# Loading the first 512 rows already transposed: the head of a fused attention and gate kernel

## The chip, the cores and the metric

The kernel runs on one core of a Trainium2 chip. The metric is the device time of one execution in microseconds (us). The engines that matter are TensorE (PE: matrix products; its weight loads are listed as PEld), VectorE (DVE), ScalarE (ACT), GpSimd (POOL), and SyncE (SP), which issues most DMAs. ACT issues some DMAs too; its DMA queue is called ACTq in the trace, that of SP SPq.

## The reference

A layer normalization of x (2048 rows of 512) feeds two branches: attention of 32 heads of 128 against cached keys and values, and a gated product. The two results are multiplied and added to x.

```python
xn = _layernorm(x, axis=-1)          # (x - mean) / sqrt(var + eps)
# A: q = xn @ wq ; softmax(q k^T / sqrt(128)) v ; @ wo            -> s
# B: gate = xn @ W_gate ; up = xn @ W_up                          (512 -> 1792)
#    h = gate * (gate > 0) * up ; h @ W_down                      (1792 -> 512)
# g = silu(B)
return x + s * g
```

All tensors are bfloat16. The weights of the gated branch have 1792 columns, that is 14 chunks of 128.

## The kernel before

The 2048 rows of x are handled as four quarters of 512 rows (Q = 0 to 3), each of four tiles of 128 rows. A matrix product on TensorE needs its inputs with the contracted dimension on the partitions, so x has to be transposed: 512 features as four blocks of 128 partitions.

The kernel starts with the gated branch of quarter 0. There are two ways to a transposed input. For quarter 0, in a hurry, the kernel uses the head: it only subtracts the mean, and puts the row factor 1/sqrt(var + eps) in later (r2 and r2h, line 571 and line 575, used after the down product: gate and up each carry one such factor, so the result carries its square). For the attention branch and the other quarters, VectorE takes statistics (`ln_stats`, line 419; `ln_aggr`, line 424), ACT the square root (`ln_sqrt`, line 431), VectorE the coefficients (`ln_coef`, lines 436 and 439), GpSimd normalizes (`ln_norm`, line 445), and SP transposes each normalized tile by DMA into `xnT` (line 557).

The order of all instructions is written out by hand; each engine works through its own list, and semaphores (`_wait`, `sig`) tie the lists together. No planner moves anything in this part.

At the start SP and ACT issue the loads: the four tiles of quarter 0 one by one (`load_x0`, line 328), the gate and up weights in four column groups (`load_w`, line 322, chunk limits 0, 2, 5, 9, 14), the other quarters of x (`load_xq`, line 332), and the down weights (line 350). TensorE meanwhile runs 18 products of ones with ones (`warm_mm`, line 475).

The head (`head_ln`, line 505) then goes tile by tile. For one tile: VectorE takes statistics and subtracts the mean (`head_center`, lines 450 to 454), TensorE transposes four blocks through PSUM (line 486 for the first tile, line 462 for the others), ACT copies them to `xcT` (line 493, line 467), and TensorE multiplies the tile with the first two weight chunks, gate and up, 16 matmuls of 128 columns (line 502 for the first tile, line 541 for the others).

The chunks 2 to 13 of quarter 0 follow in `emit_gate_up` (line 705): per chunk four matmuls of 512 columns for gate (line 729) and four for up (line 733); ACT applies the ReLU (line 689), VectorE multiplies (line 693), and `ln_task(fc)` (line 561) is called once for each chunk: it puts one piece of the statistics of the other quarters behind the product on VectorE. A chunk's PSUM banks come from a ring of three pairs (the pair of chunk 2 lies in the accumulator banks), and go back when VectorE's product has read them. Then comes the down product of quarter 0 (`emit_down`, line 832), which waits product by product for VectorE, the gate and up chunks of quarter 2, and the attention, which fills the rest of the time. When the last quarter is normalized, `issue_first` (line 373) issues the first keys, values and query weights on SP, behind the 16 transposes of line 557.

Of the kernel before, what the change touches and what calls it, by code (L numbers as in the profile page):

```python
# [8 lines left out]
ALU = mybir.AluOpType  # L9
# [43 lines left out]
def bass_recurrent_scan__mha_block_cached__glu_gated_reglu__prompt_kernel(  # L53
# [12 lines left out]
    _, S, D = A_x.shape  # L66
# [6 lines left out]
    QB = S // NQ  # L73
    NT = S // 128
    DC = D // 128
# [30 lines left out]
    x2 = A_x[0]  # L106
# [4 lines left out]
    pe = nc.tensor  # L111
# [5 lines left out]
    with ExitStack() as es:  # L117
# [201 lines left out]
        def load_w(eng, dst, src, sems, k):  # L319
            a, b_ = FCS[k] * 128, FCS[k + 1] * 128  # L320
            if b_ > a:
                sems[k].sig(eng.dma_start(dst[:, :, a:b_], src[:, :, a:b_]))

        x0_tok = {}
        x_tok = {}

        def load_x0(eng, n):
            x0_tok[n] = sem_x0[n].sig(eng.dma_start(x_sb[:, n:n + 1, :], x_t[:, n:n + 1, :]))

        def load_xq(Q):  # L330
            x_tok[Q] = sem_x[Q].sig(
                sp.dma_start(x_sb[:, 4 * Q:4 * Q + 4, :], x_t[:, 4 * Q:4 * Q + 4, :]))
# [40 lines left out]
        def issue_first():  # L373
            issue_kt(0)
            issue_wq(0)
            issue_v(0)
            issue_v(1)
            issue_wq(1)
            issue_wo(0)
            if NG > 1:  # L380
                issue_wo(1)
# [30 lines left out]
            ring_order.insert(1, s)  # L412

        def ln_stats(n):
            if n < 4:
                _wait(dve, x0_tok[n])
            elif n % 4 == 0:
                _wait(dve, x_tok[n // 4])
            return sem_ln1.sig(dve.bn_stats(stats[:, n, :], x_sb[:, n, :]))

        def ln_aggr(ns, stok):
            _wait(dve, stok)
            for n in ns:
                atok = sem_ln2.sig(dve.bn_aggr(mv[:, n, :], stats[:, n, :]))
            return atok

        def ln_sqrt(ns, atok):
            a, b_ = ns[0], ns[-1] + 1
            _wait(act, atok)
            return sem_sq.sig(  # L430
                act.activation(sqv[:, a:b_, :], mv[:, a:b_, 1:2], ACTF.Sqrt, bias=eps_sb[:]))
# [15 lines left out]

        xt_ready = {Q: [] for Q in range(QB)}

        def head_center(n):  # L450
            atok = ln_aggr([n], ln_stats(n))
            _wait(dve, atok)
            return sem_ln4.sig(
                dve.tensor_scalar(xc_sb[:, n, :], x_sb[:, n, :], mv[:, n, 0:1], None, op0=ALU.subtract))

        def head_transpose(n, ntok):
            tp_ps = acc_bf[n % 2]
            _wait(pe, acc_free[n % 2])
            _wait(pe, ntok)
            ins = None  # L460
            for c in range(DC):
                ins = pe.transpose(tp_ps[:, c * 128:(c + 1) * 128],
                                   xc_sb[:, n, c * 128:(c + 1) * 128], ident[:])
            ptok = sem_tp.sig(ins)
            src = tp_ps[:, 0:DC * 128].rearrange("p (c q) -> p c q", c=DC)
            _wait(act, ptok)
            acc_free[n % 2] = sem_xa.sig(act.copy(xcT[:, :, n * 128:(n + 1) * 128], src))
            return acc_free[n % 2]

        ones_w = nc.const_aps.tensor(1.0, [128, 128], BF16)  # L470
        ones_r = nc.const_aps.tensor(1.0, [128, 256], BF16)

# [1 line left out]
            for _i in range(k):  # L474
                pe.matmul(ps_r[:, 2 * NSLOT - 1, 0:256], ones_w, ones_r, start=True, stop=True)

        def head_first_transpose(ntok):
            toks = []
            for k in range(2):
                if k == 0:  # L480
                    _wait(pe, tok_pool)
                    _wait(pe, ntok)
                ins = None
                for i in range(DC // 2):
                    c = k * (DC // 2) + i
                    ins = pe.transpose(acc_bf[k][:, i * 128:(i + 1) * 128],
                                       xc_sb[:, 0, c * 128:(c + 1) * 128], ident[:])
                toks.append(sem_tp.sig(ins))
            for k in range(2):
                _wait(act, toks[k])  # L490
                src = acc_bf[k][:, 0:DC * 64].rearrange("p (c q) -> p c q", c=DC // 2)
                acc_free[k] = sem_xa.sig(
                    act.copy(xcT[:, k * (DC // 2):(k + 1) * (DC // 2), 0:128], src))
            return list(acc_free)

        def head_first_tile(k, i):
            W, sems = ((Wg_sb, sem_wg), (Wu_sb, sem_wu))[i]
            if k == 0:
                pe.wait_ge(sems[0].h, 16)
            for fc in range(HFC):  # L500
                for c in range(k * (DC // 2), (k + 1) * (DC // 2)):
                    pe.matmul(ps_r[:, 2 * half_slots[fc] + i, 0:128], W[:, c, fc * 128:(fc + 1) * 128],
                              xcT[:, c, 0:128], start=(c == 0), stop=(c == DC - 1))

        def head_ln():
            c0 = head_first_transpose(head_center(0))
            warm_mm(3)
            n1 = head_center(1)
            n2 = head_center(2)
            n3 = head_center(3)  # L510
            for _i in range(HFC):
                half_slots.append(ring_acquire())
            _wait(pe, c0[0])
            head_first_tile(0, 0)
            c1 = head_transpose(1, n1)
            head_first_tile(0, 1)
            _wait(pe, c0[1])
            head_first_tile(1, 0)
            head_first_tile(1, 1)
            c2 = head_transpose(2, n2)  # L520
            _wait(pe, c1)
            head_tile(1, 0)
            head_tile(1, 1)
            c3 = head_transpose(3, n3)
            _wait(pe, c2)
            head_tile(2, 0)
            head_tile(2, 1)
            _wait(pe, c3)
            head_tile(3, 0)
            head_tile(3, 1)  # L530

        half_slots = []

        def head_tile(n, fc):
            hs = slice(n * 128, (n + 1) * 128)
            fs = slice(fc * 128, (fc + 1) * 128)
            s = half_slots[fc]
            for i, W in enumerate((Wg_sb, Wu_sb)):
                ins = None
                for c in range(DC):  # L540
                    ins = pe.matmul(ps_r[:, 2 * s + i, hs], W[:, c, fs], xcT[:, c, hs],
                                    start=(c == 0), stop=(c == DC - 1))
                if n == 3:
                    half_tok[(fc, i)] = (sem_gate if i == 0 else sem_gu).sig(ins)
# [5 lines left out]
        def ln_finish(Q):  # L550
            ns, sqtok = ln_hold.pop("sq")
            ctok = ln_coef(ns, sqtok)
            for n in ns:
                ntok = ln_norm(pool, sem_nm, n, ctok)
                _wait(sp, ntok)
                xt_tok = sem_xq[Q].sig(
                    sp.dma_start_transpose(xnT[:, :, n * 128:(n + 1) * 128], xn_sb[:, n, :]))
            xt_ready[Q] = [xt_tok]
            return ctok

        def ln_task(i):
            if i < 4 * (QB - 1):
                if i == 1:
                    ns = list(range(4))
                    ln_hold["sq"] = (ns, ln_sqrt(ns, sem_ln2.cur()))
                ln_hold["st"] = ln_stats(4 + i)
                if i == 2:
                    ctok = ln_finish(0)
# [7 lines left out]
                if i % 4 == 3:  # L576
                    ns = list(range(i + 1, i + 5))
                    ln_hold["sq"] = (ns, ln_sqrt(ns, ln_aggr(ns, ln_hold["st"])))
                elif i >= 4 and i % 4 == 0:
                    ln_finish(i // 4)  # L580
            elif i == 4 * (QB - 1):
                ln_finish(QB - 1)
                issue_first()

        HS = S // 2
        HC = DC // 2
# [1457 lines left out]
```

## Time and profile before

| | us |
|---|---|
| median of 3 runs | 1241.56 (1241.18 to 1241.78) |
| the profiled execution | 1241.5 |
| its span, first to last instruction | 1239.9 |
| TensorE busy | 1232.4 (99%) |
| ACT busy | 1039.6 (84%) |
| VectorE busy | 876.3 (71%) |
| GpSimd busy | 729.8 (59%) |

The profile is one execution, taken by the hardware profiler. Its page gives the busy time of each engine, the span in slices, the DMA queues, the chain of work that ended last (followed back from the last instruction to what released each step), and the costliest groups of instructions. Further views answer questions: the timeline lists instructions in order (start, length, engine, line, operation, output and inputs, and in brackets how long the engine was idle before and who released it); the view of waits lists who waited for whom, with total, number of times and longest; the view of DMAs lists each issue with its size and the median time from its issue to its landing; the view of stretches gives busy times, granted clock, share of the DMA engines and GB/s of chosen stretches. Times in these rows are microseconds from the start of the span. Matmuls are pipelined: four that are listed with 1.03 us together follow the next ones 0.86 us later.

### The profile page before, as it was taken

To read this page: it belongs to the slowest core of one execution; us is meant where nothing else is said; L and a number is where in the kernel's file an instruction comes from. 1 tells how busy PE (TensorE), PEld (TensorE's weight loads), DVE (VectorE), ACT (ScalarE), POOL (GpSimd) and SP (SyncE) were. 2 spreads that over 40 slices of the span, in tenths; PEclk is the share of its full clock that TensorE was granted. 3 is DMA by queue.
4 is the path that set the end of the run, shared out by engine and by line. 5 is a ranking of instruction groups with operands and counts; after the bars stand their busy time and mean duration, and the time that the engine had idled before them with its cause. 6 is when DMAs were issued, how large, how long until landed. Compare 5 with 4: busy or idle time off the path is not lost.

```text
span 1239.9 us, 29084 instructions
## 1 busy us (share of the span) xinstructions
PE 1232.4 (99%) x11933; PEld 817.3 (66%) x11933; DVE 876.3 (71%) x1314; ACT 1039.6 (84%) x1108; POOL 729.8 (59%) x839
## 2 busy tenths in 40 slices
PE   9999999999999999999999999999999999999998
PEld 5466666776666666666666666666666666666664
DVE  6668788667676767676776777676677677675587
ACT  3457877668898998989989999989998999989994
POOL 3355876313757556745866566846765576662367
PEclk9999999999999999999999999999999999999999
DMA  9712431323222332233122322234222232238526
GB/s 276 157 31 37 79 79 23 52 48 98 53 49 52 65 70 52 48 69 63 38 35 52 73 61 53 48 69 69 48 52 57 39 56 48 52 69 141 112 37 143
DMA packets 279027, 85.38 MB, mean 69 GB/s; under 512 B 253552, under 2 KB 278896, under 8 KB 278896
## 3 DMA queue, kind: packets, MB, share of 16 engines
q1 hardware_dynamic: 277120, 82.08, 34.2%
q8 instruction: 95, 1.56, 0.6%
q10 hardware_dynamic: 1776, 1.44, 0.4%
q14 instruction: 36, 0.29, 0.1%
HBM read 36.96 MB, written 4.19 MB: 33 GB/s over the span
## 4 chain that ended last, share of the span: by engine, by line
PE 96%; POOL 1%; DVE 1%; issue 1%; DMA 0%; ACT 0%; POOLq 0%; DVEq 0%
PE ps_acc L1676 37%; PE ps_r L1567 35%; PE ps_r L1050 5%; PE ps_r L1167 3%; PE ps_r L1406 3%; PE ps_r L1228 3%; PE ps_r L1466 2%; PE ps_r L914 2%; PE ps_r L729 2%; PE ps_r L733 2%; PE ps_acc L832 1%; PE ps_r L1497 1%; PE ps_r L1498 0%; POOL gT L1755 0%; POOL s_acc L1533 0%
## 5 line engine op out<-in xcount | busy, mean ns | idle before, releaser
L1579 ACT ACTIVATE PT<-ps_r 128x1024 bf16<-128x1024 f32 x1024 | 988.7, 1025 | 129.6 <-PE ps_r L1567 117.5
L1676 PEld LDWEIGHTS ps_acc<-V_sb,PT 128*128 128x128 bf16 x8192 | 545.1, 98 | 231.1 <-issue 29.6
L1676 PE MATMUL ps_acc<-V_sb,PT 128*128 128x129 bf16 x8192 | 632.2, 220 | 0.0
L1567 PE MATMUL ps_r<-QT_sb,KT_sb 128*128 128x512 bf16 x2048 | 605.1, 379 | 0.2 <-DVE s_acc L1386 0.2
L1055 DVE TENSOR_TENSOR UVR<-UVR,ps_r 128x512 f32<-128x512 f32 (+1 forms) x228 | 168.7, 756 | 85.2 <-PE ps_r L1050 83.0
L1376 DVE TENSOR_TENSOR s_acc<-s_acc,ps_r 128x1024 f32<-128x1024 f32 x130 | 156.8, 1219 | 32.6 <-PE ps_r L1406 22.5
L1567 PEld LDWEIGHTS ps_r<-QT_sb,KT_sb 128*128 128x128 bf16 x2048 | 161.2, 98 | 26.4 <-DVE UVR L1055 4.3
L1015 POOL TENSOR_TENSOR TI<-xn_sb 128x512 f16<-128x512 f16 x48 | 55.9, 1165 | 97.0 <-PE ps_r L1050 97.0
L1384 DVE TENSOR_TENSOR s_acc<-s_acc,ps_r 128x512 f32<-128x512 f32 x116 | 77.4, 686 | 22.0 <-PE ps_r L1466 17.8
L1599 DVE TENSOR_TENSOR Onorm<-ps_acc,rz_sb 128x512 bf16<-128x512 f32 x127 | 87.8, 692 | 4.4
L1055 DVE TENSOR_TENSOR QT_sb<-UVR,ps_r 128x512 bf16<-128x512 f32 x72 | 49.5, 688 | 52.8 <-PE ps_r L1050 50.4
L1596 DVE RECIPROCAL rz_sb<-ps_acc 128x4 f32<-128x4 f32 x127 | 23.1, 182 | 82.7 <-PE ps_acc L1676 82.1
L1434 POOL TENSOR_TENSOR TI<-OX 128x512 f16<-128x512 f16 x28 | 31.8, 1156 | 65.1 <-issue 65.1
L1015 POOL TENSOR_TENSOR TI<-xnT 128x512 f16<-128x512 bf16 x36 | 41.6, 1156 | 39.7 <-PE ps_r L1050 21.4
L1322 POOL TENSOR_TENSOR WX<-Wo_sb 128x512 f16<-128x512 bf16 x7 | 8.1, 1155 | 90.4 <-DVE Wo_sb L1312 51.3
L1015 POOL TENSOR_TENSOR TI<-xn_sb,TI 128x512 f16<-128x512 f16 x48 | 56.0, 1167 | 0.0
L1123 POOL TENSOR_TENSOR QT_sb<-UVR,UVR 128x512 bf16<-128x512 f32 x24 | 29.8, 1277 | 39.9 <-DVE UVR L1055 39.9
L1050 PE MATMUL ps_r<-TI,SI 128*128 128x512 f16 x126 | 47.8, 379 | 0.0
L1123 POOL TENSOR_TENSOR UVR<-UVR,UVR 128x512 f32<-128x512 f32 x24 | 29.8, 1275 | 25.0 <-DVE UVR L1055 25.0
L1015 POOL TENSOR_TENSOR TI<-xnT,TI 128x512 f16<-128x512 bf16 x36 | 41.7, 1159 | 0.0
L1143 POOL TENSOR_SCALAR gB<-gB 128x512 bf16<-128x512 bf16 x14 | 20.8, 1485 | 30.4 <-DVE gB L1173 30.4
L1434 POOL TENSOR_TENSOR TI<-OT_store 128x512 f16<-128x512 bf16 (+1 forms) x28 | 32.1, 1170 | 8.7 <-issue 8.0
(229 smaller groups left out, 1357.8 us busy)
## 6 DMA issues: line engine op xcount, KB each, us to landing
V_sb<-in_A_v_cache_dram SPq DMA_DIRECT2D x32, 512.0 KB, 4.1
Wq_sb<-in_A_wq_dram SPq DMA_DIRECT2D x16, 256.0 KB, 3.1
Wo_sb<-in_A_wo_dram SPq DMA_DIRECT2D x8, 512.0 KB, 4.6
out_dram<-g_sb SPq DMA_DIRECT2D x4, 512.0 KB, 4.5
OT_store<-Onorm SPq DMA_TRANSPOSE x127, 2.5
Wd_sb<-in_B_W_down_dram SPq DMA_DIRECT2D x1, 1792.0 KB, 14.0
W<-in_B_W_gate_dram SPq DMA_DIRECT2D x14, 128.0 KB, 2.4
W<-in_B_W_up_dram SPq DMA_DIRECT2D x14, 128.0 KB, 2.8
```

The costliest lines, as they stand in the source:

```text
L1015: return sem_ui.sig(pool.tensor_tensor(dst, x, y, o))
L1050: return sem_up.sig(pe.matmul(dst, lhs, rhs, start=start, stop=stop, skip_group_check=True))
L1055: dve.tensor_tensor(dst, x, ps, ALU.add))
L1123: u_tok["add"] = u_tok[("add", i)] = sem_uv.sig(pool.tensor_tensor(dst, UU[:, i, :], RR[:, i, :], ALU.add))
L1167: ins = pe.matmul(ps_r[:, bank, :], L(i), R(i), start=(i == 0), stop=(i == HC - 1))
L1376: t = sem_opa.sig(dve.tensor_tensor(dst, dst, sb, op))
L1384: t = dve.tensor_tensor(dst, dst, sb, op)
L1434: return sem_oi.sig(pool.tensor_tensor(dst, x, y, o))
L1567: ins = pe.matmul(ps_r[:, 2 * s + tt, :], KT_sb[h % 2][:, t * 128:(t + 1) * 128], QT_sb[qt_slot[(h, Q)]][:], start=True, stop=True)
L1579: act.activation(PT[pb][:], ps_r[:, 2 * s:2 * s + 2, :], ACTF.Exp, scale=scale / WSC)
L1599: dve.tensor_tensor(Onorm[ob][:], o_ap, rz_sb[:].to_broadcast([128, 4, Dh]), ALU.mult))
L1676: ins = pe.matmul(o_ap, PT[pb][:, tt, j * 128:(j + 1) * 128], V_sb[vb][:, t, 0:VW], start=(t == 0 and j % 2 == 0), stop=(t == KT - 1 and j ...
```

## The change

The first 512 rows no longer come as rows for VectorE to centre. SP issues four DMA transposes, 128 rows each, from x in DRAM straight into `xcT`. TensorE multiplies each tile with a matrix of ones (four matmuls that add up in PSUM), which puts the sum over the features of each row on all partitions, and one VectorE instruction adds -1/512 of it to the tile in place. The 16 transposes on TensorE and the copies on ACT are gone, and so is the special path of the first tile. ACT now issues the first two groups of gate and up weights and then the 512 rows of x in the usual layout, which are still needed for the statistics. These statistics are moved into `ln_task`, between the chunks, where all the pieces get new places.

```diff
-        load_x0(sp, 0)
-        load_x0(act, 1)
-        load_w(sp, Wg_sb, wg_src, sem_wg, 0)
-        load_w(act, Wu_sb, wu_src, sem_wu, 0)
-        load_x0(sp, 2)
-        load_x0(sp, 3)
-        load_w(sp, Wg_sb, wg_src, sem_wg, 1)
-        load_w(sp, Wu_sb, wu_src, sem_wu, 1)
+        def load_x0t(n):
+            ts = slice(n * 128, (n + 1) * 128)
+            t0_tok.append(sem_x0[n].sig(sp.dma_start_transpose(xcT[:, :, ts], x2[ts, :])))
...
+        for n in range(4):
+            load_x0t(n)
+        for k in range(2):
+            load_w(act, Wg_sb, wg_src, sem_wg, k)
+            load_w(act, Wu_sb, wu_src, sem_wu, k)
+        load_xq(0, act)
         load_xq(1)
...
+        def head_center(n):
+            ts = slice(n * 128, (n + 1) * 128)
+            bank = n % 2
+            m_ps = ps_acc[:, bank, 0:128]
+            _wait(pe, acc_free[bank])
+            _wait(pe, t0_tok[n])
+            ins = None
+            for c in range(DC):
+                ins = pe.matmul(m_ps, ones_w, xcT[:, c, ts], start=(c == 0), stop=(c == DC - 1))
+            _wait(dve, sem_tp.sig(ins))
+            acc_free[bank] = sem_ln4.sig(
+                dve.scalar_tensor_tensor(xcT[:, :, ts], m_ps.unsqueeze(1).to_broadcast([128, DC, 128]), -1.0 / D,
+                                         xcT[:, :, ts], op0=ALU.mult, op1=ALU.add))
+            return acc_free[bank]
 
         def head_ln():
...
+            _wait(pe, tok_pool)
+            c = [head_center(0)]
             warm_mm(3)
+            c.append(head_center(1))
             for _i in range(HFC):
                 half_slots.append(ring_acquire())
+            for k in range(2):
+                pe.wait_ge((sem_wg, sem_wu)[k][0].h, 16)
+            for n in range(4):
+                _wait(pe, c[n])
+                head_tile(n, 0)
+                head_tile(n, 1)
+                if n < 2:
+                    c.append(head_center(n + 2))
...
         def ln_task(i):
+            for n in ((0,), (1,), (2, 3), (4,), (5,), (6,), (7,), (8, 9), (10,), (11,), (12,), (13,), (14, 15), ())[i]:
+                ln_hold["st"] = ln_stats(n)
+                if n % 4 == 3:
+                    ns = list(range(n - 3, n + 1))
+                    ln_hold["ag", n // 4] = (ns, ln_aggr(ns, ln_hold["st"]))
+            if i in (4, 8, 11, 13):
+                ns, atok = ln_hold.pop(("ag", (4, 8, 11, 13).index(i)))
+                if i == 4:
+                    _wait(act, warm_tok)
+                ln_hold["sq"] = (ns, ln_sqrt(ns, atok))
+            if i in (5, 9, 12, 13):
+                Q = (5, 9, 12, 13).index(i)
+                ctok = ln_finish(Q)
+                if Q == 0:
                     _wait(dve, ctok)
...
+                if Q == QB - 1:
+                    issue_first()
```

More of the change, by code (lines that the diff above doesn't have):

```diff
@@ L322, in load_w, with load_xq @@
                 sems[k].sig(eng.dma_start(dst[:, :, a:b_], src[:, :, a:b_]))
-        x0_tok = {}
         x_tok = {}
-        def load_x0(eng, n):
-            x0_tok[n] = sem_x0[n].sig(eng.dma_start(x_sb[:, n:n + 1, :], x_t[:, n:n + 1, :]))
-        def load_xq(Q):
-            x_tok[Q] = sem_x[Q].sig(
-                sp.dma_start(x_sb[:, 4 * Q:4 * Q + 4, :], x_t[:, 4 * Q:4 * Q + 4, :]))
-        load_x0(sp, 0)
-        load_x0(act, 1)
-        load_w(sp, Wg_sb, wg_src, sem_wg, 0)
-        load_w(act, Wu_sb, wu_src, sem_wu, 0)
-        load_x0(sp, 2)
-        load_x0(sp, 3)
-        load_w(sp, Wg_sb, wg_src, sem_wg, 1)
-        load_w(sp, Wu_sb, wu_src, sem_wu, 1)
+        t0_tok = []
+        def load_x0t(n):
+            ts = slice(n * 128, (n + 1) * 128)
+            t0_tok.append(sem_x0[n].sig(sp.dma_start_transpose(xcT[:, :, ts], x2[ts, :])))
+        def load_xq(Q, eng=sp):
+            x_tok[Q] = sem_x[Q].sig(
+                eng.dma_start(x_sb[:, 4 * Q:4 * Q + 4, :], x_t[:, 4 * Q:4 * Q + 4, :]))
+        for n in range(4):
[4 more added lines that the diff above has]
+        load_xq(0, act)
         load_xq(1)
@@ L414, in ln_stats @@
         def ln_stats(n):
-            if n < 4:
-                _wait(dve, x0_tok[n])
-            elif n % 4 == 0:
+            if n % 4 == 0:
                 _wait(dve, x_tok[n // 4])
@@ L448, in bass_recurrent_scan__mha_block_cached__glu_gated_reglu__prompt_kernel @@
         xt_ready = {Q: [] for Q in range(QB)}
[L450 to L468, printed above, removed]
         ones_w = nc.const_aps.tensor(1.0, [128, 128], BF16)
@@ L475, in warm_mm @@
                 pe.matmul(ps_r[:, 2 * NSLOT - 1, 0:256], ones_w, ones_r, start=True, stop=True)
[L477 to L503, printed above, removed]
+        def head_center(n):
[12 more added lines that the diff above has]
+            return acc_free[bank]
@@ L575, in ln_task @@
                         dve.tensor_scalar(r2h[:], r2[:], 0.5 / YSC, None, op0=ALU.mult))
[L576 to L583, printed above, removed]
+                if Q == QB - 1:
+                    issue_first()
         HS = S // 2
```

29 lines of the change are left out of this document (removed).

## The prediction

> **What bounds the kernel now.** First the page: span, busy times and the chain that ended last.
>
> ```profile
> span 1239.9 us, 29084 instructions
> PE 1232.4 (99%) x11933; PEld 817.3 (66%) x11933; DVE 876.3 (71%) x1314; ACT 1039.6 (84%) x1108; POOL 729.8 (59%) x839
> PE 96%; POOL 1%; DVE 1%; issue 1%; DMA 0%; ACT 0%; POOLq 0%; DVEq 0%
> ```
>
> TensorE is busy 1232.4 of 1239.9 us and carries 96% of the chain: whatever shifts TensorE's start shifts the end by as much, as long as no later wait opens. The profiled execution took 1241.5 us (1.6 us outside its span); the median of the three runs, 1241.56 us, is the same for this purpose, so I add the change to 1241.5.
>
> Second, that chain in the first 80 us, and who kept TensorE waiting there (columns: start, length, what; then engine, line, releaser, total, times, longest).
>
> ```profile
> 0.72 2.98 DMA x_sb<-in_A_x_dram
> 9.17 1.79 PE ps_r L541 x32
> 10.96 0.86 PE ps_acc L729 x4
> 31.68 12.09 PE ps_acc L832 x56
> ...
> PE ps_acc L486 <- DVE xc_sb L454: 0.7, 1, 0.7
> PE ps_acc L462 <- DVE xc_sb L454: 0.2, 1, 0.2
> ```
>
> After the head, TensorE waits for nobody: chunks 2 to 13 of the gate run back to back, 12 x 1.73 = 20.7 us from 10.96 to 31.68, then the 56 matmuls of the down product. Only the head has slack to win, and its prices are in the timeline of the first 12 us.
>
> ```profile
> 1.15 0.47 ACTq L322 DMA_DIRECT2D Wu_sb<-in_B_W_up_dram  x1
> 0.76 3.71 PE L475 MATMUL ps_r<-const-bfloat16-1.0 128*128 128x256 bf16 x18 [0.76 <-PEq L2029]
> 3.72 0.69 DVE L419 BATCH_NORM_STATS2 stats<-x_sb 128x6 f32<-128x512 bf16 x1 [3.72 <-DMA x_sb<-in_A_x_dram]
> 4.67 0.35 DVE L454 TENSOR_SCALAR xc_sb<-x_sb,mv 128x512 bf16<-128x512 bf16 x1
> 5.17 0.38 PE L486 MATMUL ps_acc<-ident,xc_sb 128*128 128x128 bf16 x4 [0.70 <-DVE xc_sb L454]
> 5.47 0.65 ACT L493 COPY xcT<-ps_acc 128x256 bf16<-128x256 bf16 x2 [2.33 <-PE ps_acc L486]
> 5.90 0.40 PE L502 MATMUL ps_r<-xcT,Wg_sb 128*128 128x128 bf16 x4
> 6.79 0.59 ACT L467 COPY xcT<-ps_acc 128x512 bf16<-128x512 bf16 x1 [0.67 <-PE ps_acc L462]
> 10.80 1.03 PE L729 MATMUL ps_acc<-xcT,Wg_sb 128*128 128x512 bf16 x4
> 11.03 0.69 DVE L693 TENSOR_TENSOR hT<-gr_sb,ps_r 128x512 bf16<-128x512 bf16 x1 [2.39 <-PE ps_r L541]
> ```
>
> The head ends at 10.80, when the full-width chunk starts. Before that the first tile goes landing 3.72, statistics, centering, transposes 5.17, copy 5.47, product 5.90: 2.2 us.
>
> **The change, step by step.**
>
> Removed: four statistics/centering groups (DVE), 16 transposes (TensorE), five copies (ACT). Added: 16 matmuls with ones, of the transposes' size (0.38 for four, pipelined; I take 0.25 in a stream), and four DVE subtractions from PSUM. The subtraction is not in the trace. Ends: 0.35 (the old centering, SBUF only) and 0.69 (L693, the same 128x512 with one PSUM operand); it has that PSUM operand, so 0.69. From landing to a usable tile this is 0.25 + 0.1 + 0.69 = 1.05 us, 1.1 less than the 2.2. The tiles' products stay: 32 in 1.79 us, so 0.9 us per tile of 16.
>
> So everything hangs on when the four transposes land. Their nearest rows: SBUF transposes of the same 128x512 (line 557: min/median/max of the issue in ns, then landing in us), and transposes beside a big transfer of ACT's queue at the kernel's end.
>
> ```profile
> L557 SPq DMA_TRANSPOSE xnT<-xn_sb x16: 1264/1265/5744, 15.9 to 41.7; - x16
> DMA to landing us min/median/max: 2.5/2.6/10.7
> ...
> FO<-gT SPq DMA_TRANSPOSE x2, 2.5
> ...
> 1230.04 0.40 ACTq L1723 DMA_DIRECT2D out_dram<-FO  x1
> 1230.39 1.93 SPq L1719 DMA_TRANSPOSE FO<-gT  x1
> ```
>
> The DMA rows that go with it, the loads' rows, and stretches (bounds in us, busy time of the five engines, granted clock, share of the DMA engines, GB/s):
>
> ```profile
> out_dram<-FO ACTq DMA_DIRECT2D x1, 512.0 KB, 3.9
> FO<-gT SPq DMA_TRANSPOSE x1, 4.1
> ...
> Wu_sb<-in_B_W_up_dram SPq DMA_DIRECT2D x1, 512.0 KB, 8.5
> Wu_sb<-in_B_W_up_dram ACTq DMA_DIRECT2D x1, 256.0 KB, 3.8
> Wg_sb<-in_B_W_gate_dram SPq DMA_DIRECT2D x1, 256.0 KB, 4.1
> Wd_sb<-in_B_W_down_dram SPq DMA_DIRECT2D x1, 1792.0 KB, 14.0
> ...
> 1.00:2.00 1.00, 1.00 (x7) 0.69 (x6) 0.00 (x0) 0.35 (x1) 0.51 (x4) 1.00 0.19 37
> 2.00:3.00 1.00, 1.00 (x6) 0.74 (x5) 0.00 (x0) 0.99 (x2) 0.00 (x0) 1.00 0.86 251
> ...
> 4.50:10.80 6.30, 5.38 (x84) 4.76 (x85) 3.90 (x11) 2.88 (x6) 0.00 (x0) 1.00 1.09 337
> 1130.00:1135.00 5.00, 5.00 (x55) 3.47 (x54) 2.56 (x4) 4.43 (x6) 3.04 (x3) 1.00 1.19 217
> ```
>
> A lone transpose costs SP 1.27 us and lands 2.5 us after its issue began. The one issued at 1230.39, beside a 512 KB transfer that ACT had issued 0.35 us earlier, held SP 1.93 us and landed after 4.1. In the changed kernel ACT issues 256 + 256 + 384 + 384 + 512 KB at once, 1.83 MB, which at the 337 GB/s of that stage is 5.4 us of full DMA: the transposes run in just that company. Ends for them: 1.27 apart and 2.5 to land (7.0 for the fourth: 0.72 + 3 x 1.27 + 2.5), or waiting until ACT's queue is empty (below). I take the row with a big neighbour for all but the first, whose issue starts before any packet flows: issues at 0.72, 1.99, 3.92, 5.85, landings at about 4, 6.1, 8.0, 9.95.
>
> TensorE's order (written by hand) is: mean 0, three warm-ups, mean 1, wait for both weights, tile 0, mean 2, tile 1, mean 3, tile 2, tile 3. The weights are issued at 0.71 and 1.15 on ACT and land at about 5.0 (0.47 us of issue each, 3.8 to land, as before). Then: warm-up to 4.47; mean 0 to 4.85, subtraction to 5.6; mean 1 waits for 6.1, to 6.35; tile 0 to 7.3; mean 2 waits for 8.0, to 8.3; tile 1 to 9.2; mean 3 waits for 9.95, to 10.2; tile 2 to 11.1; tile 3, whose subtraction ended at 11.0, to 12.0. That is 12.0 against 10.80: **+1.2 us**. Each mean in TensorE's queue holds the tile behind it, although that tile's own operands are ready.
>
> With the undisturbed landings the same walk ends at 9.75 (-1.05), because then tiles follow each other from 5.65.
>
> Statistics of the first 512 rows move into the chunks, with the x they read loaded last on ACT. Here DVE's rhythm decides:
>
> ```profile
> 20.00 0.69 DVE L419 BATCH_NORM_STATS2 stats<-x_sb 128x6 f32<-128x512 bf16 x1
> 20.60 0.67 DVE L693 TENSOR_TENSOR hT<-gr_sb,ps_r 128x512 bf16<-128x512 bf16 x1
> 23.10 0.38 DVE L424 BATCH_NORM_AGGREGATE mv<-stats 128x2 f32<-128x6 f32 x4
> ...
> ACT sqv L431 <- DVE mv L424: 7.3, 3, 2.8
> 4.91 1.15 SPq L322 DMA_DIRECT2D Wu_sb<-in_B_W_up_dram  x1
> 12.06 1.42 SPq L350 DMA_DIRECT2D Wd_sb<-in_B_W_down_dram  x1
> ```
>
> DVE starts one such operation every 0.6 us. After the first product it owes 13 products and 16 statistics (29 x 0.6 = 17.4), four aggregations (0.5 each) and the coefficient pairs (1.6): 21 us. With the head's end at 12.0 it begins near 12.8 and is through by 33.8; the last product is needed by the fourteenth down matmul, at 12.0 + 20.7 + 13 x 0.216 = 35.5. So it costs nothing, hidden by 1.7 us of slack; with a late x it would be next in line. ACT's three waits for aggregations (7.3 us) go, but they cost TensorE nothing and give nothing back. GpSimd normalizes the quarters later, SP's 16 transposes of them (1.27 each) then end near 44 instead of 43, before the differences on DVE need them at 46.2.
>
> Loads: the first 512 rows are fetched twice, 0.52 MB more, 1.6 us of DMA at 337 GB/s for all behind, and SP reaches its other loads only after the fourth transpose, at 7.8. Before, the third weight group was in by 13.4 (4.91 + 8.5). Now SP's next x and this group (1.57 MB, 4.7 us) are in by about 14, and chunk 5 needs it at 10.96 + 3 x 1.73 = 16.1, or later with a later head. The down weights landed at 26.1 (12.06 + 14.0), come 1.6 later, and are needed at 31.7. Covered; without that cover the 1.6 would show. ACT's table load slips behind five issues, to about 3, and ACT has nothing to do before 11.
>
> **Weighed against the skill.** The Trainium skill, Advanced Engine Details and Errata, section X-Bar Transpose (TRN2), calls transposing DMAs as fast as plain ones, 350 to 400 GB/s; transposes from DRAM at 1130 to 1135 moved 217. By the page the four would take 1.5 us of DMA instead of 2.4, an estimate that changes only the last rival.
>
> **Rivals.**
>
> Fair sharing. If the transposes share the DMA engines evenly with the weights, all 0.52 + 1.31 MB are through 5.4 us after the first packets (about 2.1: 37 GB/s flow from 1 to 2 us, 251 from 2 to 3), and the fourth lands near 8.0. Mean 3 ends at 8.3, its subtraction at 9.1, tile 3 at 10.0: -0.8 us, **1240.7**. For it: Wg on SP and Wu on ACT, issued together, took 4.1 and 3.8 us, an even split. Against it: the 4.1 us transpose. The Trainium skill, DMA: Bandwidth & Descriptors, section Queues, rings and completion order, has each DMA engine take packets from the queues in turn; by that this case would hold, and the even split agrees, the late transpose hardly.
>
> Starved transposes (the other side). If the 1230.39 row means that a transpose moves only when ACT's queue has drained, ACT's 1.83 MB keep it until 2.1 + 5.4 = 7.5; then four at 217 GB/s, 0.6 us each, land at 8.6, 9.2, 9.8, 10.4. Mean 0 ends at 8.9, tile 0 starts at 9.75, and with means and tiles behind each other tile 3 ends at 13.85: +3.05 us, **1244.55**. TensorE then idles from 4.85 to 8.65; its first 18 matmuls of 256 columns took 3.71 us, 0.206 each, where 512 columns later take 0.216, so a fall back to that pace for the next 3.4 us adds up to 2.5: 1247. It decides from a fourth landing of about 11.2, or from a fallback.
>
> The shorter path buys nothing: with weights landing at 5.9 instead of 5.0, tile 0 would start where it did, and even undisturbed transposes would save only what the tiles behind it wait less, some 0.8 us; that gives 1240.7 too and is counted with sharing.
>
> **How the numbers follow.** Likeliest (0.38): 1241.5 + 1.2 = 1242.7, own range 1241.7 to 1244.2, a twentieth of all chances beyond the bound. Sharing 0.22; starved 0.33; a stall opened later by DVE or a load, over 2.5 us, 0.05; an unforeseen gain 0.02 (the head allows no more than 1.75: 16 means and 64 products at 0.056 after weights at 5.0). About 0.2%, 2.5 us, is what a measurement of this kernel can tell from no change. Faster 0.02, same 0.33 + 0.22 = 0.55, slower 0.05 + 0.33 + 0.05 = 0.43. The range runs from just under the sharing case to within the starved one: 1240.4 to 1246.4.
>
> **What would show it.** Right: the third and fourth transposes held 1.9 us on SP and landing about 4 us after issue; TensorE waiting for them before means 1 to 3; the full-width chunk at 12.0; the chunks after it again 20.7 us without waits; subtractions of 0.69. Wrong: landings of 2.5 (then 9.75 to 10.0), landings only after x on ACT's queue (then 13.85), or a wait of TensorE on DVE or a load in the chunks.

## The result, and the profile after

| | before | after |
|---|---|---|
| median of six runs each, same chip, us | 1241.59 (1241.18 to 1241.78) | 1247.69 (1246.27 to 1248.48) |
| the profiled execution, us | 1241.5 | 1246.27 |
| its span, us | 1239.9 | 1244.8 |

The kernel became slower: ratio 1.0048, 95% interval 1.0037 to 1.0059, some 6 us. The prediction was 1242.7 with a range up to 1246.4. The profiled execution of after is the fastest of its six runs, so its trace accounts for 4.9 us of span. The page of after says the same of the bound as that of before: span, busy times, and the chain that ended last.

```profile
span 1244.8 us, 29080 instructions
PE 1234.4 (99%) x11933; PEld 818.9 (66%) x11933; DVE 876.4 (70%) x1314; ACT 1037.5 (83%) x1103; POOL 730.3 (59%) x839
PE 94%; POOL 2%; SPq 1%; DMA 1%; DVE 1%; issue 1%; ACT 0%; POOLq 0%; DVEq 0%; ACTq 0%
```

TensorE is still the bound, busy 2.0 us longer, though it has the same number of instructions. The rest is waiting, and the view of TensorE's waits in the first 80 us (total, times, longest) says for whom.

```profile
PE ps_acc L462 <- DMA xcT<-in_A_x_dram: 3.5, 2, 1.8
PE ps_r L682 <- DVE hT L646: 0.4, 1, 0.4
```

The timeline of the head shows where these lie (start, length, what; in brackets the idle time before and its cause).

```profile
0.72 5.23 SPq L329 DMA_TRANSPOSE xcT<-in_A_x_dram  x4
0.76 4.00 PE L452 MATMUL ps_r<-const-bfloat16-1.0 128*128 128x256 bf16 x18 [0.76 <-PEq L1982]
2.87 0.60 ACTq L333 DMA_DIRECT2D x_sb<-in_A_x_dram  x1
...
6.59 0.58 PE L462 MATMUL ps_acc<-xcT,const-bfloat16-1.0 128*128 128x128 bf16 x4 [1.84 <-DMA xcT<-in_A_x_dram]
7.21 0.69 DVE L465 SCALAR_TENSOR_TENSOR xcT<-ps_acc,xcT 128x512 bf16<-128x512 f32 x1 [7.21 <-PE ps_acc L462]
9.43 0.61 PE L462 MATMUL ps_acc<-xcT,const-bfloat16-1.0 128*128 128x128 bf16 x4 [1.61 <-DMA xcT<-in_A_x_dram]
9.83 0.63 PE L493 MATMUL ps_r<-xcT,Wg_sb 128*128 128x128 bf16 x4
10.26 0.63 PE L493 MATMUL ps_r<-xcT,Wu_sb 128*128 128x128 bf16 x4
12.68 0.39 PE L493 MATMUL ps_r<-xcT,Wg_sb 128*128 128x128 bf16 x4
12.90 0.39 PE L493 MATMUL ps_r<-xcT,Wu_sb 128*128 128x128 bf16 x4
15.20 1.03 PE L682 MATMUL ps_acc<-xcT,Wg_sb 128*128 128x512 bf16 x4
```

The first full-width chunk starts at 15.20 instead of 10.80: **4.40 of the 4.9 us are lost in the head.** TensorE waits for the first transpose until 6.59 and for the second until 9.43. After that it never waits again in the head, but from 9.83 to about 12.4 four matmuls of 128 columns follow each other every 0.43 us (9.83, 10.26) and only then every 0.22 (12.68, 12.90). Most of the longer busy time comes from this.

The view of DMAs gives the time from issue to landing. The transposes are rows 1, 2, 3 and 6 (issued at 0.72, 2.08, 3.38 and 4.68).

```profile
xcT<-in_A_x_dram SPq DMA_TRANSPOSE x1, 5.7
xcT<-in_A_x_dram SPq DMA_TRANSPOSE x1, 7.3
xcT<-in_A_x_dram SPq DMA_TRANSPOSE x1, 7.9
Wu_sb<-in_B_W_up_dram ACTq DMA_DIRECT2D x1, 256.0 KB, 4.2
Wu_sb<-in_B_W_up_dram ACTq DMA_DIRECT2D x1, 384.0 KB, 6.9
xcT<-in_A_x_dram SPq DMA_TRANSPOSE x1, 7.1
```

They land at 6.4, 9.4, 11.3 and 11.8; ACT's two loads of Wu (issued at 1.19 and 2.30) land at 5.4 and 9.2. What the queues moved from 6 to 9 us, when all four transposes had been issued (q10 is ACT's queue, q1 that of SP: packets, MB, time as a share of 16 engines):

```profile
DMA packets 1355, 0.84 MB, mean 278 GB/s; under 512 B 497, under 2 KB 1355, under 8 KB 1355
q10 hardware_dynamic: 884, 0.72, 89.8%
q1 hardware_dynamic: 471, 0.11, 20.0%
```

The transposes' packets are small (0.11 MB in 471, some 0.23 KB each; ACT's some 0.8 KB), and they get about one packet in three. In bytes this is 0.11 of 0.83 MB, 37 GB/s, so by an estimate from these rows the 0.13 MB of one transpose take some 3.5 us; the second landed 3.0 after the first.

Another 0.57 us lie later. After the head all chunks stay 4.4 late, until the gate chunk that starts at 61.73 before and at 66.70 after (4.97 late). The first three rows are of after, from the timeline:

```profile
27.41 21.39 SPq L509 DMA_TRANSPOSE xnT<-xn_sb  x14
64.22 1.06 ACT L579 ACTIVATE W<-W 128x1024 bf16<-128x1024 bf16 x1 [2.47 <-DMA W<-in_B_W_up_dram]
66.70 1.02 PE L682 MATMUL ps_r<-xnT,Wg_sb 128*128 128x512 bf16 x4 [0.40 <-DVE hT L646]
```

and these of before:

```profile
27.63 15.30 SPq L557 DMA_TRANSPOSE xnT<-xn_sb  x11
57.96 1.06 ACT L626 ACTIVATE W<-W 128x1024 bf16<-128x1024 bf16 x1 [0.61 <-DMA W<-in_B_W_up_dram]
61.73 1.03 PE L729 MATMUL ps_r<-xnT,Wg_sb 128*128 128x512 bf16 x4
```

SP ends the transposes of normalized rows at 48.80 instead of 42.93, 5.9 later, with TensorE only 4.4 later. Behind them on SP stand keys, values, query weights, and then the weights of the next gate and up chunk (`W`), for which ACT now waits 2.47 instead of 0.61 us; ACT's ReLU stands behind that, VectorE's product behind it, and TensorE waits 0.4 for a bank.

### The profile page after: what moved, and what is told of

The parts are those of the page before. It is cut to its first block, busy times and chain, and to the rows that moved or that the text cites. A ratio compares the mean times of both kernels' runs of the same rounds, so it can differ in the third digit from the quotient of the medians.

```text
span 1244.8 us, 29080 instructions
## 1 busy us (share of the span) xinstructions
PE 1234.4 (99%) x11933; PEld 818.9 (66%) x11933; DVE 876.4 (70%) x1314; ACT 1037.5 (83%) x1103; POOL 730.3 (59%) x839
## 4 chain that ended last, share of the span: by engine, by line
PE 94%; POOL 2%; SPq 1%; DMA 1%; DVE 1%; issue 1%; ACT 0%; POOLq 0%; DVEq 0%; ACTq 0%
PE ps_acc L1629 37%; PE ps_r L1520 35%; PE ps_r L1003 5%; PE ps_r L1120 3%; PE ps_r L1359 3%; PE ps_r L1181 3%; PE ps_r L1419 2%; PE ps_r L867 2%; PE ps_r L682 1%; PE ps_r L686 1%; DMA xcT<-in_A_x_dram 1%; PE ps_r L1450 1%; POOL xn_sb L442 0%; DMA W<-in_B_W_up_dram 0%; PE ps_r L1451 0%
## 5 line engine op out<-in xcount | busy, mean ns | idle before, releaser
L642 ACT ACTIVATE gr_sb<-ps_r 128x512 bf16<-128x512 f32 x27 | 15.9, 596 | 33.7 <-PE ps_r L682 22.9
```

## The experiments

The theory was: the landing of the transposes sets the head, and they land late because ACT's queue has weights to move. Rivals: DMA transposes from DRAM are this slow by themselves; the half pace of TensorE is the loss; the moved statistics are the loss.

All results in one table, in the order in which the head ends. Landings are us from issue to landing of the four transposes. "Head end" is the start of the first full-width chunk (0.86 before the next group where its first record is missing), in brackets how much later than 10.80. "Later" are TensorE's waits between there and 80 us, and the last but one column is the span less 1239.9. The ratio is to the kernel before on the same chip.

| kernel | landings | head end | later | span | ratio, 95% interval |
|---|---|---|---|---|---|
| chunk loads first, in the kernel before | none | 10.50 (-0.3) | 0 | -0.3 | 0.9999 (0.9990 to 1.0008) |
| schedule of the statistics alone, in the kernel before | none | 10.59 (-0.2) | 1.2 | +1.1 | 1.0003 (0.9994 to 1.0012) |
| second weight group and x behind | 4.9, 3.8, 3.4, 2.8 | 11.37 (+0.6) | 2.9 | +3.8 | 1.0025 (1.0016 to 1.0035) |
| the same, loads in order | 5.0, 3.9, 3.7, 3.1 | 12.18 (+1.4) | 0 | +1.4 | 1.0010 (1.0001 to 1.0018) |
| ACT starts late | 4.1, 6.1, 5.0, 4.2 | 12.39 (+1.6) | 0 | +1.6 | 1.0023 (1.0013 to 1.0034) |
| all on one queue | 2.7, 3.7, 2.9, 2.9 | 12.65 (+1.9) | 0.2 | +2.2 | 1.0017 (1.0009 to 1.0026) |
| busy TensorE and chunk loads first | 4.8, 7.1, 7.9, 7.1 | 14.60 (+3.8) | 0 | +3.8 | 1.0035 (1.0023 to 1.0048) |
| busy TensorE | 5.9, 7.2, 8.2, 7.4 | 14.95 (+4.2) | 0.4 | +4.7 | 1.0037 (1.0025 to 1.0050) |
| chunk loads first | 4.7, 7.6, 8.1, 7.1 | 15.55 (+4.8) | 0 | +4.7 | 1.0036 (1.0023 to 1.0049) |
| the changed kernel again | 5.8, 7.9, 8.4, 7.6 | 15.68 (+4.9) | 0.4 | +5.4 | 1.0044 (1.0031 to 1.0056) |
| x behind | 5.9, 7.4, 6.6, 5.5 | 15.74 (+4.9) | 0.3 | +5.4 | 1.0049 (1.0035 to 1.0062) |
| transposes alone | 2.5, 2.7, 2.8, 2.9 | 24.51 (+13.7) | 1.8 | +15.8 | 1.0121 (1.0107 to 1.0135) |

In every row the head's delay and the later waits add up to the span within 0.3 us. So these two terms are what a profiled execution loses, within that 0.3. ACT's load order, the packets and the half pace act only through them.

**Transposes alone.**

```diff
         for n in range(4):
             load_x0t(n)
+        _wait(act, t0_tok[3])
         for k in range(2):
```

> The changed kernel, but ACT issues its weights and x only after the fourth transpose has landed, so that the transposes have the DMA engines to themselves. If they are late in the changed kernel because they share the engines with ACT's 1.83 MB (theory), they now land 2.5 to 3 us after their issues, the fourth near 7.5. If transposes from DRAM are slow by themselves (rival), they still take 5.7 to 7.8 us. The weights come late by construction, near 10 to 11, so the kernel itself gains nothing: 1246 to 1250 us by both.

With nothing beside them the transposes land 2.5 to 2.9 us after issue, the fourth at 7.6. So slowness by themselves is excluded. The weights then come later than expected, at 18 instead of 10 to 11: ACT issues them from 7.61 on, beside the loads that SP has begun at 6.00, and its second load (256 KB, issued at 8.15) takes 10.0. The first product waits 12.1 us for them, and the time, 1256.38, lies far above the 1246 to 1250 expected:

```profile
PE ps_r L494 <- DMA Wu_sb<-in_B_W_up_dram: 12.1, 1, 12.1
```

**Second weight group and x behind the transposes.** Only 0.5 MB of ACT's loads are left beside them.

```diff
         for n in range(4):
             load_x0t(n)
-        for k in range(2):
-            load_w(act, Wg_sb, wg_src, sem_wg, k)
-            load_w(act, Wu_sb, wu_src, sem_wu, k)
-        load_xq(0, act)
+        load_w(act, Wg_sb, wg_src, sem_wg, 0)
+        load_w(act, Wu_sb, wu_src, sem_wu, 0)
+        load_w(sp, Wg_sb, wg_src, sem_wg, 1)
+        load_w(sp, Wu_sb, wu_src, sem_wu, 1)
+        load_xq(0)
```

> The changed kernel, but only the first weight group (256 + 256 KB) stays on ACT; the second group and the 512 rows of x go on SP's queue behind the transposes. If the delay grows with the bytes that ACT has queued (theory), the first transpose lands near 5 and the fourth by 8 to 9 instead of 11.8, the head ends between 10.5 and 12 instead of 15.2, and the time falls by 3 to 4 us, to 1243 to 1245. If it is SP's issue or the transposes' own pace (rival), nothing moves: 1247 to 1248.

The second transpose lands 3.8 after issue instead of 7.3 and the fourth 2.8 instead of 7.1; the head ends at 11.37. This shows the theory's first half: less on ACT's queue, earlier landings. It doesn't give the time back, since the third weight group is now late, and a chunk load once more:

```profile
PE ps_r L683 <- DMA Wu_sb<-in_B_W_up_dram: 1.9, 1, 1.9
PE ps_r L683 <- DVE hT L647: 1.0, 1, 1.0
PE ps_acc L463 <- DMA xcT<-in_A_x_dram: 1.0, 1, 1.0
```

**Busy TensorE.** More warm-up products, so that TensorE has no gap of more than 1.2 us.

```diff
-            warm_mm(3)
+            warm_mm(16)
...
-        warm_mm(18)
+        warm_mm(32)
```

> The changed kernel, with the products of ones lengthened from 18 to 32 and from 3 to 16, so that TensorE hardly idles while it waits for the first two transposes; no DMA is moved. If a part of the loss is TensorE running its tiles at half pace after idling (theory), 128-column matmuls keep 0.056 us from the first tile on, and the time falls by 0.9 us at least (what the profiled execution lost), more in executions that lost more: 1245.5 to 1247. If the pace has nothing to do with idling (rival), the time stays at 1247 to 1248.

The half pace is gone (four matmuls of 128 columns every 0.22 us from the first tile), the landings are as late as ever, and the head ends at 14.95, 0.25 before the profiled execution of the changed kernel and 0.7 before that of its repetition. The time that the faster matmuls save goes in part into a new wait for a later transpose:

```profile
9.30 0.40 PE L462 MATMUL ps_acc<-xcT,const-bfloat16-1.0 128*128 128x128 bf16 x4 [0.36 <-DMA xcT<-in_A_x_dram]
11.76 0.38 PE L462 MATMUL ps_acc<-xcT,const-bfloat16-1.0 128*128 128x128 bf16 x4 [1.17 <-DMA xcT<-in_A_x_dram]
```

So the half pace is a part of the loss and not its cause; with it the third and fourth landings are hidden, without it they show.

**Schedule of the statistics alone.** The kernel before, with the head as it was, and with only the later places of the quarters' statistics and normalizations in `ln_task`.

```diff
-            if i < 4 * (QB - 1):
-                if i == 1:
-                    ns = list(range(4))
-                    ln_hold["sq"] = (ns, ln_sqrt(ns, sem_ln2.cur()))
-                ln_hold["st"] = ln_stats(4 + i)
...
+            for n in ((), (), (), (4,), (5,), (6,), (7,), (8, 9), (10,), (11,), (12,), (13,), (14, 15), ())[i]:
+                ln_hold["st"] = ln_stats(n)
...
+            if i in (5, 9, 12, 13):
+                Q = (5, 9, 12, 13).index(i)
+                ctok = ln_finish(Q)
...
```

> The kernel before with its old head and loads, and of the change only the new places of the later statistics, square roots and normalizations in the chunks. If the later normalizations push back SP's transposes and the loads behind them until ACT stalls on a weight load (theory, read from the changed kernel's 0.56 us between chunks 10 and 11 of the third quarter), the time rises by 0.3 to 0.7 us, to 1241.9 to 1242.3, with the same stall near 62. If the new places are hidden, as the prediction had it (rival): 1241.6, no wait.

The median is 0.34 us up (1241.67 against 1241.33), which the interval doesn't separate from nothing. But its profiled execution, 1242.76, the slowest of its eleven runs, has the later wait with the same cause: ACT waits 3.25 for the chunk's weights, TensorE 1.18.

```profile
60.39 1.06 ACT L630 ACTIVATE W<-W 128x1024 bf16<-128x1024 bf16 x1 [3.25 <-DMA W<-in_B_W_up_dram]
62.87 1.02 PE L733 MATMUL ps_r<-xnT,Wg_sb 128*128 128x512 bf16 x4 [1.18 <-DVE hT L697]
```

So the schedule brings these loads to the edge of being late: once in eleven executions a microsecond. The other ten have no trace; their spans are at most 0.4 us over 1239.9.

**Chunk loads first**, in the changed kernel and in the kernel before: the loads of two chunks go ahead of the second values, query and output weights on SP.

```diff
             issue_v(0)
+
+        def issue_rest():
             issue_v(1)
...
         gu_load(1)
+        issue_rest()
```

> The changed kernel; on SP, behind the first keys, query weights and values, the two pairs of gate and up chunks for the next stage (128 KB each) go ahead of the second values, the second query weights and the two output weights. Theory: the wait of ACT on such a chunk (2.5 us, near 61.8) and TensorE's wait behind it (near 66) come only from these loads being late on SP, and both vanish; the span loses 0.56 us (that execution's loss there), the head stays at 15.2: 1246.8 to 1247.3 where the changed kernel had 1247.7. Rival (the stall has another cause, or is made up later): no change, 1247.7.

> The kernel before, with the order of loads on SP alone changed (the two pairs of chunks ahead of the second values and the weights). ACT's wait there was 0.6 us and TensorE had none, so both theories have it at the time before, 1241.3 to 1241.6; it shows whether the reordering costs or brings anything by itself.

In the changed kernel the later wait is gone and TensorE waits for nothing but transposes:

```profile
PE ps_acc L464 <- DMA xcT<-in_A_x_dram: 3.7, 2, 2.9
```

The ratio falls to 1.0036, which doesn't separate from the changed kernel's interval. In the kernel before it is worth nothing (0.9999), as there that wait didn't exist.

**The same as the second, loads in order**: the second weight group and x behind the transposes, the third group ahead of the next x, and chunk loads first.

```diff
...
+        load_w(act, Wg_sb, wg_src, sem_wg, 0)
+        load_w(act, Wu_sb, wu_src, sem_wu, 0)
+        load_w(sp, Wg_sb, wg_src, sem_wg, 1)
+        load_w(sp, Wu_sb, wu_src, sem_wu, 1)
+        load_xq(0)
         load_w(sp, Wg_sb, wg_src, sem_wg, 2)
         load_w(sp, Wu_sb, wu_src, sem_wu, 2)
+        load_xq(1)
...
```

> As the run with the rest behind the transposes, with two more edits: the third weight group comes before the second quarter of x on SP, and the order of loads on SP of the run just above. Theory: that run's waits after the head (0.3 us for the second weight group, 1.9 us for the third, 1.0 us behind ACT's late chunk) fall to at most 0.3 + 0.4 + 0, and the time by 2 to 2.6 us, to 1242.0 to 1242.5. Rival (DVE, whose statistics now come later, is next in line): a wait on DVE of 1 us or more before the down product, and 1243 to 1244.

It is the fastest of all the versions with transposing loads, 1242.59 against 1241.41 (1242.0 to 1242.5 was expected), ratio 1.0010 where the changed kernel has 1.0044. All later waits are gone, and TensorE waits only for the first transpose:

```profile
PE ps_acc L465 <- DMA xcT<-in_A_x_dram: 1.1, 1, 1.1
```

Yet its head ends 0.8 later than that of the run without the new order, although the landings agree within 0.3. After nearly the same wait for the first transpose, TensorE ran at full pace there (first row, 0.38 for four matmuls) and here at half pace until about 8.9 (second and third row). The edits change nothing that early, so this is a difference between executions, and a head end read from a single trace can move by that much:

```profile
5.76 0.38 PE L463 MATMUL ps_acc<-xcT,const-bfloat16-1.0 128*128 128x128 bf16 x4 [1.01 <-DMA xcT<-in_A_x_dram]
5.83 0.58 PE L465 MATMUL ps_acc<-xcT,const-bfloat16-1.0 128*128 128x128 bf16 x4 [1.07 <-DMA xcT<-in_A_x_dram]
8.98 0.39 PE L465 MATMUL ps_acc<-xcT,const-bfloat16-1.0 128*128 128x128 bf16 x4
```

**All on one queue.** The first transpose, the first weight group, the other transposes, and the rest, all on SP; ACT issues none of these. The second mean goes between the halves of the first tile.

```diff
+        load_x0t(0)
+        load_w(sp, Wg_sb, wg_src, sem_wg, 0)
+        load_w(sp, Wu_sb, wu_src, sem_wu, 0)
+        for n in range(1, 4):
             load_x0t(n)
...
+        load_w(sp, Wg_sb, wg_src, sem_wg, 1)
+        load_w(sp, Wu_sb, wu_src, sem_wu, 1)
+        load_xq(0)
...
```

> As the run just above, but no weights on ACT: SP's queue holds the first transpose, the first weight group, the other three transposes, then the rest, so that no transpose shares the DMA engines with another queue; TensorE takes the second mean between the two halves of the first tile. Theory (transposes in one queue keep their 2.5 to 3 us): landings near 3.3, then the weights near 5, then 5.7, 7, 8.3; the head ends near 10.3 to 10.8 and the time is 1241 to 1242, no slower than before by more than 0.1%. Rival (another queue is not needed for the delay): transposes of 4 us and more, and 1243 or more.

No transpose takes over 3.7 us, and TensorE waits for none; it waits for weights instead, 1.0 for the first group and 1.5 for the second, and the time is 1243.60 where 1241 to 1242 was expected:

```profile
PE ps_acc L687 <- DMA Wu_sb<-in_B_W_up_dram: 1.5, 1, 1.5
PE ps_r L498 <- DMA Wu_sb<-in_B_W_up_dram: 1.0, 1, 1.0
```

**x behind.** Only the 512 rows of x go from ACT to SP, behind the transposes.

```diff
-        load_xq(0, act)
+        load_xq(0)
```

> The changed kernel; both weight groups stay on ACT (1.31 MB), only the 512 rows of x go behind the transposes on SP. Theory (the transposes are slow as long as ACT's queue has something to move): the first two land as in the changed kernel, about 5 to 6 and 7 us after issue, the third and fourth, which there ended with x at 11.2 and 11.8, by 9.5 to 10; the head ends near 13 to 13.5 and the time falls by 1.5 to 2 us, to 1245.5 to 1246.5. Rival (x on ACT does not matter): 1247.7.

A miss for the theory as I had put it. The third and fourth transposes do land earlier (10.0 and 10.2 instead of 11.3 and 11.8), yet the time is the same, 1.0049 beside 1.0044. The second still lands at 9.5, beside the second weight group, and everything after it is one run of half-pace matmuls that covers the later landings:

```profile
9.57 0.61 PE L462 MATMUL ps_acc<-xcT,const-bfloat16-1.0 128*128 128x128 bf16 x4 [1.56 <-DMA xcT<-in_A_x_dram]
13.38 0.44 PE L493 MATMUL ps_r<-xcT,Wu_sb 128*128 128x128 bf16 x4
15.74 1.03 PE L682 MATMUL ps_acc<-xcT,Wg_sb 128*128 128x512 bf16 x4
```

So it is the second landing, with the half pace behind it, that sets the head, and what delays that landing is the weights, not x.

**Busy TensorE and chunk loads first together, with the changed kernel again beside it.**

> The changed kernel with the longer products of ones and the earlier loads of the next chunks together. Theory: the half pace (0.9 us and more) and the late chunk (0.56) are separate losses and add up; what is left is the late landing of the transposes, 3 to 4 us over the kernel before: 1244.6 to 1245.4. Rival (TensorE waits for the same landings anyway, so that the half pace costs little): as with the earlier loads alone, 1246.1.

> The changed kernel itself, unaltered, timed beside the three runs of this group so that they can be compared on one chip: 1247.7 us by every theory, with landings of the transposes between 4.7 and 8.1 us after their issues.

The first run has the two edits shown above, the second has none. The unaltered kernel came to 1246.76 here and to 1247.69 in its first six runs, so its medians agree within 1 us only. Together the two edits take 1.5 us off the median (1245.21 against 1246.76), though the intervals of the ratios, 1.0035 and 1.0044, overlap. In the profile a head of +3.8 us is left and nothing else: with TensorE at full pace and the later wait gone, those 3.8 are what the late transposes cost by themselves in this execution, in which TensorE has its second transpose at 9.21 and not at 10.07 as in the repetition. x behind and a busy TensorE were not tried together.

**ACT starts late.** ACT issues its weights only after its table load, and the second half of the second group and x go on SP; the second mean between the halves of the first tile, chunk loads first.

```diff
...
+        _wait(act, eps_tok)
+        load_w(act, Wg_sb, wg_src, sem_wg, 0)
+        load_w(act, Wu_sb, wu_src, sem_wu, 0)
+        load_w(act, Wg_sb, wg_src, sem_wg, 1)
+        load_w(sp, Wu_sb, wu_src, sem_wu, 1)
+        load_xq(0)
...
```

> An attempt at a kernel that is faster than both: four transposes on SP from the start, ACT begins its loads 0.8 us later and carries only the first weight group and the gate half of the second (0.92 MB), the up half and the 512 rows of x go behind the transposes; the second mean lies between the halves of the first tile; loads of the next chunks early. If the first transpose then lands before ACT's traffic, near 3.5, and the weights near 5.5: head end 10.3 to 11, time 1241 to 1242. If each later transpose still meets ACT's weights: landings of 4 to 6 us, head end 12 to 13, 1242.5 to 1244.

The first transpose gets through in 4.1, the second, now beside the weights, takes 6.1 again. The head ends at 12.39, and the time is 1244.2 against 1241.3, just past the second of the two cases expected (1242.5 to 1244). No version of the study beats the kernel before.

## Why the prediction was wrong

*The landings: the step that failed.* The prediction took landings of about 4 us beside ACT's traffic, from the one row at 1230.39, and had SP held 1.93 us by each after the first: landings at 4, 6.1, 8.0 and 9.95. Measured: SP is held 1.3 us by each (5.23 for four), and they land 5.7 to 7.9 after issue, at 6.4, 9.4, 11.3 and 11.8. The nearest row had 512 KB for a neighbour; here it was 1.31 MB of weights and then x. With 0.5 MB (second weight group behind) the first took 4.9, near the row. The size of the neighbour's traffic was the term that the row couldn't give. From the second landing to the head's end the walk needed 5.9 us, and 5.77 were measured; that these are so close is luck, since 1.4 us of half pace (seven groups 0.2 longer each) took the place of the walk's two waits for the third and fourth landing (0.7 and 0.75). So of the miss in the head, 15.20 against 12.0, 3.3 is the second landing alone, 9.43 against 6.1.

*The rivals.* Fair sharing of the bytes is excluded: a fourth landing of 8.0 was its condition, 11.8 came. The Trainium skill, DMA: Bandwidth & Descriptors, section Queues, rings and completion order, has each DMA engine take packets from the queues in turn. The packets of the profile went 884 to 471 from 6 to 9 us, not one to one, though its packets need not be those of the page; with x behind they went 599 to 600 from 6 to 8.4 us. The split is thus not a fixed one, and the larger part of the loss in bytes is that the transposes' are a third as large. Starved transposes came nearest, with landings of 8.6, 9.2, 9.8 and 10.4: the second was right to 0.2, but the first got through early and the last two came some 1.5 later, so the transposes weren't shut out, they got little. That rival named a fourth landing of 11.2, or a fall to half pace, as the point from which the case decides; both occurred. Its time with half pace, 1247, lies 0.7 under the measured median, in part by luck: 3.4 us at half pace lose 1.7 and not 2.5, which gives 1246.25. The landings of both rivals also hold 0.5 us that their sums don't name (7.5 + 0.6 is 8.1, not 8.6). In the bound for a gain, 80 matmuls of 0.056 from 5.0 on end at 9.5, which allows 1.3 and not 1.75.

*The half pace.* Foreseen only inside that rival, at up to 2.5 us; it took 1.4.

*TensorE's order by hand, each mean holding the tile behind it.* Right: the first tile's own operand was ready at 7.90 (7.21 + 0.69) and its weights at 5.4, and it began at 9.83.

*Means and subtraction.* Right: 0.69 for each subtraction, with nothing else on VectorE around it. A mean takes 0.22 in a stream at full pace, near the 0.25 assumed, and 0.43 at half pace.

*Statistics between the chunks at no cost.* Right for VectorE: no wait of TensorE for a product in quarter 0, the chunks back to back.

*SP's transposes of the normalized quarters, "near 44 instead of 43, before the differences at 46.2".* Wrong: 48.80. Of the 4.8 us over 44, 3.2 are the later head (4.4 instead of 1.2) and 1.6 the step's own. It also looked only at the differences. The loads that stand behind them on SP, and ACT's and VectorE's work behind those, were left out; that cost 0.57 us in the profiled execution, and with the chunk loads first the wait is gone. The schedule alone puts it at the edge.

*Loads covered.* Right in the changed kernel, where nothing waited for the third weight group or the down weights; the late head gave them more room.

*The sum.* 1.2 predicted; in the profiled execution 4.4 + 0.57. The median of the changed kernel is 1.4 us above its profiled execution. What its other runs lose more has no trace and stays open. The four slowest list a mean granted clock of 0.996, the profiled one 0.999; by an estimate from 0.996 (0.004 of 1247 us, at half clock) that is some 10 us at half clock, so a longer half pace would fit. But in the repetition and with the chunk loads first, the runs at 0.996 and 0.997 are not the slower ones.

## What to carry to other kernels

A transfer's time in an empty stretch is a lower end, and a row with a neighbour holds for that neighbour's size only: ask how many bytes the other queue has outstanding, and in what packets, for as long as the transfer lives. When an engine works through an order written by hand, find the one landing on which its queue stands still, here the second of four, and price that; the later ones may be hidden behind it. A step that is moved on one queue delays everything behind it on that queue, so follow the queue to its end and not to the first consumer.

## What the runs showed that was not expected

- The same 128x512 transpose from DRAM lands 2.5 to 2.9 us after issue alone, 2.8 to 4.9 beside 0.5 MB of the other queue, 5.5 to 7.4 beside 1.3 MB (x behind) and 5.7 to 7.9 beside 1.8 MB (4.7 to 8.4 over the five traces with that load). On the issuing engine it costs 1.3 us in all four.
- Together the queues move less. From 5 to 11 us (the busy times of the five engines, clock, DMA share, GB/s), first before, then after:

```profile
5.00:11.00 6.00, 5.58 (x84) 4.86 (x85) 3.43 (x10) 3.08 (x7) 0.00 (x0) 1.00 1.09 340
```

```profile
5.00:11.00 6.00, 2.79 (x22) 2.28 (x23) 1.38 (x2) 0.00 (x1) 0.00 (x0) 1.00 1.18 268
```

  The DMA engines are busy throughout in both, with 340 and 268 GB/s.
- TensorE ran at half pace (0.107 us for a matmul of 128 columns instead of 0.056) after two gaps of 1.84 and 1.61 us, with the granted clock shown as 1.00. The column doesn't prove full pace at the start: it shows 1.00 also beside the 18 warm-up products, which take some 0.21 each for 256 columns, that is half pace too. Later it does follow the pace. In the kernel with the transposes alone TensorE has nothing to do from 6.15 to 18.26; the column falls to 0.50 at 9.4, and four matmuls of 128 columns take 0.43 from 18.26 on until both change at about 23.0. The Trainium skill, TensorE: Matmul & The Clock Gate, section Part 1: The HAM clock gate (the "warmup" mystery), has full speed come about 3.4 us into sustained work; from 9.43 to about 12.4 is 3 us and from 18.26 to 23.0 is 4.7, which agrees as an order. Full pace had probably not been reached before the gaps: in the kernel in which ACT starts late, the same 18 warm-up products took the same 4.00 us, and with a gap of only 0.22 the next four matmuls were still slow, those from 6.44 on fast (the rows below). The length of the gap doesn't decide it alone: of the two kernels with the second group and x behind, one was at full pace after 1.01 us of waiting, the other not after 1.07.

```profile
4.98 0.58 PE L466 MATMUL ps_acc<-xcT,const-bfloat16-1.0 128*128 128x128 bf16 x4 [0.22 <-DMA xcT<-in_A_x_dram]
6.44 0.38 PE L498 MATMUL ps_r<-xcT,Wg_sb 128*128 128x128 bf16 x4 [0.23 <-DVE xcT L469]
```

- The changed kernel's six runs spread over 2.2 us, those of the kernel before over 0.6.
